# Softmax exponentials over three and two PSUM banks by turns, and VectorE's score tiles on a bank of their own

## Chip, cores, metric

One core of one Trainium2 chip. The metric is the device time in microseconds of one execution, the median of several. A run is called slow here when it is over 1.5% above the fastest of the same kernel; ratios use the other runs alone.

## The reference, cut to what matters

Two branches are mixed by a gate: a long convolution (done as a Fourier transform by matrix products) and attention with 32 query heads of size 20 over one shared key and value head. S = 2048, D = 640.

```
g = sigmoid((x * gate_w).sum(-1))
a = q * (irfft(rfft(kv) * rfft(ssm_k)) + kv * ssm_D)         # kv = shift_conv(k) * v
scores = einsum("bhqd,bkd->bhqk", q, k) * 20 ** -0.5         # 32 heads, 2048 x 2048
b = (softmax(scores) @ v).reshape(...) @ wo
out = g * a + (1 - g) * b
```

The exponentials, 32 x 2048 x 2048 of them, set the time. The convolution's matmuls are "side work", placed into TensorE's gaps. "Filler" matmuls multiply zeros and change no result; the program puts them into gaps that are left, and they are meant to keep TensorE's clock up.

## The kernel before

The program lists all operations with their dependencies; a scheduler in Python then makes a fixed order for each engine from estimated costs. TensorE executes that order strictly. Score tiles are 128 keys x 512 queries of one head, one PSUM bank each; four heads (r = 0 to 3) sit in the four row groups of 32 partitions, so four score matmuls run at once: one "burst". A PV matmul multiplies exponentials by values; PV matmuls also come in bursts, with one matmul for each head.

```python
SLACK = 0.2          # how far a side matmul may overshoot the next main burst's ready time
FILL = 0.5           # filler matmuls are placed while TensorE's busy share is below this
DVE_J = [()] * 5 + [(2, 9)] * 27     # in 27 of 32 groups, half of two key blocks' tiles go to VectorE

def busy_in(self, t, w):             # share of the last w us; `active` has one span per op
    ...                              # of cost > 0.05: a burst's last matmul, 0.25 us
# in pick_pe, when no side group fits:
    if (... self.can_fill and gap > 0.1 and self.busy_in(t, 2.4) < FILL):
        f = Op("pe", self.filler, c_mm(512), "c", "fill", 0.0)

def pairs(u):                        # ring of three pairs of banks, 0 to 5
    return (2 * u) % 3, (2 * u + 1) % 3
def QK(u, rs=(0, 1, 2, 3)): ...      # four score matmuls: one burst
def EXP(u, h):
    p, slot = pairs(u)[h], (2 * u + h) % 5          # five exp buffers
    if h == 1 and on_dve(u):
        return DEXP(u, p)                           # VectorE reads the ring's pair
    e.activation(ET[slot], ps[:, 1024 * p:1024 * p + 1024], ACT.Exp, scale=SCALE)
def PV(u): ...                       # four matmuls into bank 6, one per head
# order: EXP(u,0)  QK(u+1)  EXP(u,1)  PV(u-1)  ...      side work: bank 7
```

## Time and profile before

| | before |
|---|---|
| time, median of the 3 runs at first (range) | 930.93 us (928.56 to 932.95) |
| ScalarE busy | 97% of 928 us |
| exponentials | 970 of 128x1024 |
| score bursts | 566 (458 of four tiles, 108 of two) |
| filler matmuls during attention | 213, 67 us |
| first exponential starts, last ends | 25.5 us, 917.2 us |

The lines of the page and the chain in order of time are in the prediction and are not repeated.

### The profile page before, as it was taken

To read this page: it belongs to the slowest core of one execution; us is meant where nothing else is said; L and a number is where in the kernel's file an instruction comes from. 1 tells how busy PE (TensorE), PEld (TensorE's weight loads), DVE (VectorE), ACT (ScalarE), POOL (GpSimd) and SP (SyncE) were. 2 spreads that over 40 slices of the span, in tenths; PEclk is the share of its full clock that TensorE was granted. 3 is DMA by queue.
4 is the path that set the end of the run, shared out by engine and by line. 5 is a ranking of instruction groups with operands and counts; after the bars stand their busy time and mean duration, and the time that the engine had idled before them with its cause. 6 is when DMAs were issued, how large, how long until landed. Compare 5 with 4: busy or idle time off the path is not lost.

```text
span 928.0 us, 16257 instructions
## 1 busy us (share of the span) xinstructions
PE 804.4 (87%) x6836; PEld 333.9 (36%) x6836; DVE 615.4 (66%) x808; ACT 903.9 (97%) x994; POOL 390.3 (42%) x331
## 2 busy tenths in 40 slices
PE   6877778888998898999898899889999989888886
PEld 3222113443444333444243344333443433332222
DVE  5667884566776676776677667667657666667554
ACT  5999999999999999999999999999999999999995
POOL 2970001768724258723268325468324872000000
PEclk9999999999999999999999999999999998999898
DMA  7722542001000001000001010000000003021000
GB/s 159 256 77 85 190 130 65 13 9 40 18 19 18 13 16 33 19 19 18 18 14 30 20 53 19 18 13 9 17 19 18 13 13 95 26 69 49 20 13 28
DMA packets 40406, 41.18 MB, mean 44 GB/s; under 512 B 20147, under 2 KB 33581, under 8 KB 40333
## 3 DMA queue, kind: packets, MB, share of 16 engines
q1 hardware_dynamic: 38067, 39.56, 13.9%
q8 instruction: 53, 0.87, 0.4%
q10 hardware_dynamic: 2266, 0.59, 0.3%
q14 instruction: 20, 0.16, 0.1%
HBM read 31.76 MB, written 6.02 MB: 41 GB/s over the span
## 4 chain that ended last, share of the span: by engine, by line
ACT 93%; PE 5%; DMA 1%; SPq 1%; DVE 0%; DVEq 0%; issue 0%
ACT ET L972 93%; PE ps L956 1%; PE ps L1405 1%; PE ps L998 1%; DMA xT<-in_A_q_dram 1%; SPq L671 1%; PE ps L842 0%; PE ps L1318 0%; PE ps L898 0%; PE ps L1116 0%; PE ps L1123 0%; PE ps L1254 0%; DVE outsb L1138 0%; ACT L747 0%; PE ps L856 0%; DVEq L446 0%
## 5 line engine op out<-in xcount | busy, mean ns | idle before, releaser
L972 ACT ACTIVATE ET<-ps 128x1024 bf16<-128x1024 f32 x970 | 890.3, 1213 | 2.4 <-PE ps L956 2.0
L956 PE MATMUL ps<-qT,kT 21*128 21x512 bf16 x2048 | 224.4, 388 | 104.9 <-ACT ET L972 95.5
L1285 POOL TENSOR_TENSOR Pp<-X,K 128x512 f32<-128x512 bf16 x120 | 170.3, 1446 | 276.7 <-DVE K L1273 276.7
L998 PE MATMUL ps<-ET,vaug 128*32 128x512 bf16 x1940 | 210.0, 394 | 1.0 <-ACT ET L972 1.0
L956 PEld LDWEIGHTS ps<-qT,kT 21*128 21x128 bf16 x2048 | 56.2, 91 | 273.0 <-ACT ET L972 266.0
L986 DVE TENSOR_SCALAR dJ<-ps 128x1024 uint32<-128x1024 f32 x54 | 66.1, 1223 | 47.3 <-PE ps L956 47.2
L998 PEld LDWEIGHTS ps<-ET,vaug 128*32 128x32 bf16 x1940 | 52.3, 93 | 116.6 <-issue 112.5
L1285 POOL TENSOR_TENSOR AB<-Pp 128x256 bf16<-128x256 f32 x80 | 84.4, 1055 | 5.9
L991 DVE SCALAR_TENSOR_TENSOR dE<-dJ,dE 128x1024 f32<-128x1024 uint16 x54 | 79.4, 1471 | 0.4
L994 DVE SCALAR_TENSOR_TENSOR ETd<-dJ,dE 128x1024 bf16<-128x1024 f32 x54 | 78.1, 1446 | 0.8
L1318 PE MATMUL ps<-AB,Tcos 128*128 128x256 bf16 x320 | 76.2, 275 | 1.0 <-DVE K L1273 0.9
L993 DVE SCALAR_TENSOR_TENSOR dJ<-dJ 128x1024 f32<-128x1024 uint16 x54 | 75.1, 1391 | 0.8
L1405 PE MATMUL ps<-Tcos,zeros 128*128 128x512 bf16 x213 | 70.8, 409 | 0.0
L1318 PE MATMUL ps<-AB,Tsin 128*128 128x256 bf16 x280 | 67.3, 274 | 0.0
L1285 POOL TENSOR_TENSOR Pp<-Pp 128x512 f32<-128x512 f32 x40 | 61.3, 1532 | 3.1
L1265 DVE TENSOR_SCALAR X<-ps 128x512 bf16<-128x512 f32 x35 | 24.1, 690 | 47.1 <-PE ps L1254 46.9
L1254 PE MATMUL ps<-ssm_kT,Tsin 128*128 128x256 bf16 x320 | 49.5, 274 | 0.0
L1254 PE MATMUL ps<-kv,Tsin 128*128 128x256 bf16 x320 | 48.2, 274 | 0.0
L1254 PE MATMUL ps<-kv,Tcos 128*128 128x256 bf16 x320 | 46.7, 275 | 1.4 <-DVE kv L1181 0.5
L989 DVE TENSOR_SCALAR dE<-dJ 128x1024 uint32<-128x1024 uint32 x54 | 46.4, 860 | 1.2
L898 PE MATMUL ps<-xT,wq_pad 128*128 128x512 bf16 x160 | 44.9, 393 | 1.4 <-DVE qT L545 1.0
L1056 DVE COPY acc<-ps 128x512 f32<-128x512 f32 x31 | 21.4, 691 | 35.9 <-PE ps L998 35.4
(136 smaller groups left out, 736.5 us busy)
## 6 DMA issues: line engine op xcount, KB each, us to landing
kslab<-in_A_k_dram SPq DMA_DIRECT2D x15, 640.0 KB, 3.6
rbc<-scr_d SPq DMA_DIRECT2D x31, 256.0 KB
scr_o<-oTn SPq DMA_DIRECT2D x24, 128.0 KB
xn<-in_A_q_dram SPq DMA_DIRECT2D x4, 640.0 KB
vslab<-in_A_v_dram SPq DMA_DIRECT2D x16, 160.0 KB, 3.6
kst<-in_A_ssm_k_dram SPq DMA_DIRECT2D x5, 512.0 KB
out_dram<-outsb SPq DMA_DIRECT2D x14, 160.0 KB
oTp<-scr_o SPq DMA_DIRECT2D x12, 160.0 KB, 3.2
```

The source lines that it names most:

```text
L956: o = op("pe", lambda e, r=r, Iu=Iu, g=g, j=j, bk=banks[r]: e.matmul(self.bank(bk), T["kT4"][32 * r:32 * r + 21, 128 * j:128 * j + 128], T ...
L972: op("act", lambda e, p=p, slot=slot: e.activation(T[f"ET{slot}"][:, :], self.ps[:, 1024 * p:1024 * p + 1024], ACT.Exp, scale=SCALE), [("p ...
L986: V(lambda e, p=p: e.tensor_scalar(J[:, :], self.ps[:, 1024 * p:1024 * p + 1024], SCALE * LOG2E * 65536.0, EOFF * 65536.0, ALU.mult, ALU.add),
L989: V(lambda e: e.tensor_scalar(E[:, :], J[:, :], 7, 0x7F800000, ALU.logical_shift_left, ALU.bitwise_and), [kJ], ["dE"], c_fast(1024), **k)
L991: V(lambda e: e.scalar_tensor_tensor(Ef, lo, ED, Ef, ALU.add, ALU.mult), [kJ, "dE"], ["dE"], c_ps(1024), **k)
L993: V(lambda e: e.scalar_tensor_tensor(Jf, lo, EP, lo, ALU.add, ALU.mult), [kJ], [kJ], c_ps(1024), **k)
L994: V(lambda e: e.scalar_tensor_tensor(T["ETd"][:, :], Jf, EQ, Ef, ALU.add, ALU.mult), [kJ, "dE"], ["ETd"], c_ps(1024), **k)
L998: return op("pe", lambda e, r=r, j=j, src=src: e.matmul(self.bank(6)[32 * r:32 * r + 32, :], T["vaug"][:, j, :], src[:, 512 * (r % 2):512 ...
L1254: o = self.mm(gr, lambda e, bk, lhs=lhs, rhs=rhs, comp=comp, n=n: e.matmul(self.bank(bk, 256, 256 * comp), lhs, rhs, start=(n == 0), stop= ...
L1285: f = lambda e: e.tensor_tensor(out, a, b, alu)
L1318: self.mm(gr, lambda e, bk, lhs=lhs, fc=fc, comp=comp, h=h: e.matmul(self.bank(bk, 256, 256 * h), lhs, AB[:, fc, :, comp, :], start=(fc == ...
L1405: sch.filler = lambda e: e.matmul(self.bank(6), self.T["zeros"][:, :], self.T["Tcos"][:, 0, 0:512], start=False, stop=False)
```

## The change

The intent: each exponential instruction has a fixed cost, so fewer, wider ones save time. Six ring banks for three pairs become five, read as 3 and 2 by turns. VectorE's tiles leave the ring; their matmuls "ride" along with a score burst in a row group that is free, into bank 5 or 7, which side work shares. The five exp buffers of 1024 become two of 1536 and two of 1024, in the same memory. The two or three tiles of one exponential are called a unit.

```diff
+PATIENCE = 3.0
+SIDE = (7, 5)
-def group(self, name, prio, banks=(7,)):
+def group(self, name, prio, banks=SIDE):
-        for i in range(5):
-            sb(f"ET{i}", [128, 1024], BF16)
+        for i in range(2):
+            sb(f"ETA{i}", [128, 1536], BF16)
+            sb(f"ETB{i}", [128, 1024], BF16)
+        # stream(): all tiles in order of group G, key block j, head r, less VectorE's
+        while i < len(tiles):
+            n = 2 if len(self.units) % 2 else 3
+            self.units.append(tiles[i:i + n])
+        base = (0, 3)
+        def EXP(n):
+            lo, w = 512 * base[n % 2], 512 * len(units[n])
+            ... e.activation(et(n)[:, 0:w], self.ps[:, lo:lo + w], ACT.Exp, scale=SCALE),
+               ... [("ET", n % 4)], c_exp(w) ...
+        # DEXP: two matmuls of one tile, banks (5, 7), gr.rides = True; two VectorE reads of 512
+        # pick_pe: after a score burst, a riding group whose row is free goes first
+        for n in range(len(units)):
+            EXP(n)
+            if n + 1 < len(units):
+                QK(n + 1)
+            PVs(n - 1)        # PV groups of four tiles whose last unit is <= n - 1
```

(cut to its core)

More of the change, by code (lines that the diff above doesn't have):

```diff
@@ L24 @@
                  "cont", "nun", "succ", "ready", "start", "end", "placed", "sig", "value", "lane", "known", "seq",
-                 "banks", "last", "floating", "tail", "attached", "lat", "iss")
+                 "banks", "last", "floating", "tail", "attached", "lat", "iss", "row", "soft")
     def __init__(self, eng, fn, cost, kind, name, prio):
@@ L58, in __init__ @@
         self.iss = 0.35
+        self.row = None
+        self.soft = ()
 class Group:
     def __init__(self, banks, prio, name):
+        self.rides = False
         self.banks = banks
@@ L156, in __init__ @@
         self.active = []
+        self.rows = set()
     def busy_in(self, t, w):
@@ L191, in run @@
             op = self.pick(e, self.t[e])
-            if op is None:
+            if self.t[e] > 2000.0:
+                guard = 100001
+            if op is None or guard > 100000:
                 self.t[e] += 0.04
                 guard += 1
-                if guard > 400000:
+                if guard > 100000:
                     missing = [(o.name, o.eng) for o in g.all if not o.placed][:20]
@@ L248, in pick_pe @@
             return f
+        if self.rows and not (m is not None and m.cont):
+            best = None
+            for gr in self.gcand:
+                if gr.rides and gr.ready <= t and gr.mms[0].row not in self.rows:
+                    b = next((x for x in gr.banks if not self.bank_claimed[x] and not self.bank_busy[x]
+                              and self.bank_ready[x] <= t), None)
+                    if b is not None and (best is None or gr.prio < best[0].prio):
+                        best = gr, b
+            if best is not None:
+                gr, b = best
+                self.gcand.discard(gr)
+                gr.bank = b
+                self.bank_busy[b] = True
+                gr.mms[0].deps.update(self.bank_last[b])
+                return gr.mms[0]
         if not (m is not None and m.cont):
@@ L280, in pick_pe @@
         best = None
+        held = any(gr.rides and gr.ready <= t for gr in self.gcand)
         for gr in self.gcand:
+            if gr.rides and t - gr.ready < PATIENCE:
+                continue
             if gr.ready <= t and gr.mms[0].cost <= gap + SLACK:
@@ L284, in pick_pe @@
                 for x in gr.banks:
+                    if held and x == 5 and not gr.rides:
+                        continue
                     if not self.bank_claimed[x] and not self.bank_busy[x] and self.bank_ready[x] <= t:
@@ L305, in pick_pe @@
         _, gr, b = best
+        if gr.rides:
+            gr.mms[0].cost = 0.3
         self.gcand.discard(gr)
@@ L351, in place @@
             self.active.append((op.end - op.cost * 0.92, op.end))
+        if e == "pe":
+            if op.name != "qk":
+                self.rows = set()
+            elif op.cont:
+                self.rows.add(op.row)
+            else:
+                self.rows = {op.row}
         if op.name == "pv":
@@ L359, in place @@
                 gr.pos += 1
-                if gr.pos == len(gr.mms):
+                if gr.pos == len(gr.mms) and self.open is gr:
                     self.open = None
@@ L385, in emit @@
         for op in self.linear:
+            op.deps.difference_update(op.soft)
             drop = [d for d in op.deps if op.eng == "pe" and d.eng == "pe" and d.kind == "c"]
@@ L475, in c_fast, with c_exp @@
     return 0.16 + 0.52e-3 * n
+def c_exp(n):
+    return 0.0633 + 0.8333e-3 * n
 def c_act(n):
@@ L499, in __init__ @@
         self.crow0 = None
+        self.dqk = None
     def op(self, *a, **k):
@@ L939, in gate_fin, with stream @@
                  ["omgf"], 0.2, prio=40)
-    def attention(self, I):
+    def stream(self):
+        tiles, self.on_dve, self.pv_order = [], {}, []
+        order = (0, 1, 2, 3)
+        for G in range(8 * NB):
+            for j in range(NSC):
+                mine = order
+                if j in DVE_J[G]:
+                    mine, rest = order[:2], order[2:]
+                    self.on_dve[G, j] = tuple(sorted(rest))
+                    order = rest + mine
+                self.pv_order.append((G, j, mine))
+                tiles += [(G, j, r) for r in mine]
+        self.units, i = [], 0
+        while i < len(tiles):
+            n = 2 if len(self.units) % 2 else 3
+            self.units.append(tiles[i:i + n])
+            i += n
+        self.place_of = {t: (n, k) for n, un in enumerate(self.units) for k, t in enumerate(un)}
@@ L943, in attention, with score, et, QK @@
+    def attention(self):
         T = self.T
         op = self.op
-        N = NB * 8 * NSC
-        def pairs(u):
-            return (2 * u) % 3, (2 * u + 1) % 3
-        def QK(u, rs=(0, 1, 2, 3)):
-            Iu, g, j = u // 128, (u // 16) % 8, u % 16
-            pa, pb = pairs(u)
-            banks = (2 * pa, 2 * pa + 1, 2 * pb, 2 * pb + 1)
-            first = None
-            for r in rs:
-                o = op("pe", lambda e, r=r, Iu=Iu, g=g, j=j, bk=banks[r]: e.matmul(
-                    self.bank(bk), T["kT4"][32 * r:32 * r + 21, 128 * j:128 * j + 128],
-                    T[f"qT{Iu % 2}"][32 * r:32 * r + 21, g, :], start=True, stop=True, tile_position=(32 * r, 0)),
-                    [("kT4", j // 4), ("qT", Iu % 2, g)], [("ps", banks[r])], 0.03 if r < rs[-1] else 0.27, name="qk",
-                    main=True, cont=(r > rs[0]), banks=(banks[r],))
-                if r == rs[0]:
+        self.stream()
+        units = self.units
+        base = (0, 3)
+        started = {0}
+        def score(e, bk, G, j, r):
+            return e.matmul(self.bank(bk), T["kT4"][32 * r:32 * r + 21, 128 * j:128 * j + 128],
+                            T[f"qT{G // 8 % 2}"][32 * r:32 * r + 21, G % 8, :], start=True, stop=True,
+                            tile_position=(32 * r, 0))
+        def et(n):
+            return T["ET%s%d" % ("AB"[n % 2], n // 2 % 2)]
+        def QK(n):
+            un = units[n]
+            I = un[-1][0] // 8
+            if I not in started:
+                started.add(I)
+                self.qproj_next(I)
+                if I == NB - 1:
+                    self.g.fence(["oT3", "part"], ["xT"])
+                    self.g.fence(["wog"], ["wq_pad"])
+                    self.load_wog()
+            first = None
+            for k, (G, j, r) in enumerate(un):
+                bk = base[n % 2] + k
+                o = op("pe", lambda e, bk=bk, G=G, j=j, r=r: score(e, bk, G, j, r),
+                       [("kT4", j // 4), ("qT", G // 8 % 2, G % 8)], [("ps", bk)], 0.03 if k < len(un) - 1 else 0.27,
+                       name="qk", main=True, cont=(k > 0), banks=(bk,))
+                o.row = r
+                if k == 0:
@@ L964, in QK, with DEXP @@
                     first.deps.update(d for d in o.deps if d.eng != "pe")
-                    first.banks = tuple(banks[x] for x in rs)
-        def EXP(u, h):
-            p = pairs(u)[h]
-            slot = (2 * u + h) % 5
-            if h == 1 and on_dve(u):
-                return DEXP(u, p)
-            op("act", lambda e, p=p, slot=slot: e.activation(
-                T[f"ET{slot}"][:, :], self.ps[:, 1024 * p:1024 * p + 1024], ACT.Exp, scale=SCALE),
-                [("ps", 2 * p), ("ps", 2 * p + 1)], [("ET", slot)], 0.904, name="exp", main=True,
-                after=self.sins if u == 0 else ())
-        def DEXP(u, p):
+            first.banks = tuple(base[n % 2] + k for k in range(len(un)))
+        def EXP(n):
+            lo, w = 512 * base[n % 2], 512 * len(units[n])
+            op("act", lambda e: e.activation(et(n)[:, 0:w], self.ps[:, lo:lo + w], ACT.Exp, scale=SCALE),
+               [("ps", base[n % 2] + k) for k in range(len(units[n]))], [("ET", n % 4)], c_exp(w), name="exp", main=True,
+               after=self.sins if n == 0 else ())
+        def DEXP(G, j):
             par = self.ndexp % 2
             self.ndexp += 1
+            pr = -600.0 + 0.1 * G + 0.001 * j
             J, E, kJ = T[f"dJ{par}"], T["dE"], ("dJ", par)
@@ L983, in DEXP @@
             Ef, Jf = E[:, :].bitcast(F32), J[:, :].bitcast(F32)
-            k = dict(port=True, name="dexp", prio=-600.0 + 0.01 * u)
+            k = dict(port=True, name="dexp", prio=pr)
             V = self.dve
-            V(lambda e, p=p: e.tensor_scalar(J[:, :], self.ps[:, 1024 * p:1024 * p + 1024], SCALE * LOG2E * 65536.0,
-                                             EOFF * 65536.0, ALU.mult, ALU.add),
-              [("ps", 2 * p), ("ps", 2 * p + 1)], [kJ], c_ps(1024), prio=-8000.0, name="dexp0")
+            rs = self.on_dve[G, j]
+            for h, r in enumerate(rs):
+                gr = self.group("dqk", pr, banks=(5, 7))
+                gr.rides = True
+                w = self.g.writer.get(kJ)
+                soft = set() if h else set(self.g.readers.get(kJ, ())) | ({w} if w is not None else set())
+                self.mm(gr, lambda e, bk, r=r: score(e, bk, G, j, r), [("kT4", j // 4), ("qT", G // 8 % 2, G % 8)],
+                        0.04)
+                o = gr.mms[0]
+                o.row = r
+                if self.dqk is not None:
+                    o.deps.add(self.dqk)
+                self.dqk = o
+                o.soft = soft - o.deps
+                o.deps |= o.soft
+                self.evac(gr, "dve", lambda e, bk, h=h: e.tensor_scalar(
+                    J[:, 512 * h:512 * h + 512], self.bank(bk), SCALE * LOG2E * 65536.0, EOFF * 65536.0, ALU.mult,
+                    ALU.add), (), [kJ], c_ps(512))
             V(lambda e: e.tensor_scalar(E[:, :], J[:, :], 7, 0x7F800000, ALU.logical_shift_left, ALU.bitwise_and),
@@ L997, in PVmm @@
         def PVmm(r, j, src, key, late=False, **k):
-            return op("pe", lambda e, r=r, j=j, src=src: e.matmul(
-                self.bank(6)[32 * r:32 * r + 32, :], T["vaug"][:, j, :], src[:, 512 * (r % 2):512 * (r % 2) + 512],
+            return op("pe", lambda e: e.matmul(
+                self.bank(6)[32 * r:32 * r + 32, :], T["vaug"][:, j, :], src,
                 start=(j == 0), stop=(j == NSC - 1), tile_position=(0, 32 * r)),
                 [key, "vaug", ("vaugb", j // 4)], [] if late else [("ps", 6)], name="pv", **k)
-        def PV(u):
-            j = u % 16
-            rs = (0, 1) if on_dve(u) else (0, 1, 2, 3)
-            for r in rs:
-                slot = (2 * u + r // 2) % 5
-                o = PVmm(r, j, T[f"ET{slot}"], ("ET", slot), cost=0.03 if r < rs[-1] else 0.27, main=True,
-                         cont=(r > 0), banks=(6,))
-                o.last = j == NSC - 1
-                if j == 0:
-                    self.pv0 = o
-                if o.last and r == 0:
-                    o.deps.update(self.late_pv)
-                    self.late_pv = []
-            if on_dve(u):
-                a = PVmm(2, j, T["ETd"], "ETd", late=True, cost=0.03, after=[self.pv0])
-                b = PVmm(3, j, T["ETd"], "ETd", late=True, cost=0.27)
-                a.floating = True
-                a.tail = (b,)
-                b.deps.add(a)
-                b.attached = True
-                self.late_pv += [a, b]
@@ L1025, in on_dve @@
-        def on_dve(u):
-            return u % 16 in DVE_J[u // 16]
-        lo, hi = I * 128, I * 128 + 128
-        if I == 0:
-            QK(0)
-        for u in range(lo, hi):
-            if u + 1 < N:
-                if (u + 1) % 128 == 0:
-                    self.qproj_next(I + 1)
-            EXP(u, 0)
-            split = on_dve(u)
-            if u + 1 < N:
-                QK(u + 1, (0, 1) if split else (0, 1, 2, 3))
-            EXP(u, 1)
-            if I == 0 and u == 40:
-                self.gate_fin()
-            if u > 0:
-                PV(u - 1)
-                if u % 16 == 0:
-                    self.norm((u - 1) // 128, ((u - 1) // 16) % 8)
-            if split and u + 1 < N:
-                QK(u + 1, (2, 3))
@@ L1049, in attention, with PV @@
-        if hi == N:
-            PV(N - 1)
+        def PV(G, j, rs):
+            pv0 = None
+            for k, r in enumerate(rs):
+                n, q = self.place_of[G, j, r]
+                o = PVmm(r, j, et(n)[:, 512 * q:512 * q + 512], ("ET", n % 4), cost=0.03 if k < len(rs) - 1 else 0.27,
+                         main=True, cont=(k > 0), banks=(6,))
+                o.last = j == NSC - 1
+                if k == 0:
+                    first = o
+                    if o.last:
+                        o.deps.update(self.late_pv)
+                        self.late_pv = []
+                else:
+                    first.deps.update(d for d in o.deps if d.eng != "pe")
+            if j == 0:
+                for jd in DVE_J[G]:
+                    DEXP(G, jd)
+                    ra, rb = self.on_dve[G, jd]
+                    a = PVmm(ra, jd, T["ETd"][:, 0:512], "ETd", late=True, cost=0.03, after=[o])
+                    b = PVmm(rb, jd, T["ETd"][:, 512:1024], "ETd", late=True, cost=0.27)
+                    a.floating = True
+                    a.tail = (b,)
+                    b.deps.add(a)
+                    b.attached = True
+                    self.late_pv += [a, b]
@@ new lines, in attention, with PVs @@
+        todo = list(self.pv_order)
+        def PVs(n):
+            while todo and max(self.place_of[todo[0][0], todo[0][1], r][0] for r in todo[0][2]) <= n:
+                G, j, rs = todo.pop(0)
+                PV(G, j, rs)
+                if j == NSC - 1 and G < 8 * NB - 1:
+                    self.norm(G // 8, G % 8)
+        QK(0)
+        for n in range(len(units)):
+            EXP(n)
+            if n + 1 < len(units):
+                QK(n + 1)
+            if n == 64:
+                self.gate_fin()
+            PVs(n - 1)
@@ L1052, in norm @@
+        PVs(len(units))
     def norm(self, I, g):
@@ L1389, in build @@
         self.kshift()
-        for I in range(NB):
-            if I == NB - 1:
-                self.g.fence(["oT3", "part"], ["xT"])
-                self.g.fence(["wog"], ["wq_pad"])
-                self.load_wog()
-            self.attention(I)
+        self.attention()
         self.g.fence(self.late_fams, self.early_fams)
```

## The prediction

> **What bounds the kernel now.** I read the busy shares first, then the waits by engine, then the chain in order of time.
>
> ```profile
> PE 804.4 (87%) x6836; PEld 333.9 (36%) x6836; DVE 615.4 (66%) x808; ACT 903.9 (97%) x994; POOL 390.3 (42%) x331
> ...
> PEclk9999999999999999999999999999999998999898
> ...
> L972 ACT ACTIVATE ET<-ps 128x1024 bf16<-128x1024 f32 x970 | 890.3, 1213 | 2.4 <-PE ps L956 2.0
> L956 PE MATMUL ps<-qT,kT 21*128 21x512 bf16 x2048 | 224.4, 388 | 104.9 <-ACT ET L972 95.5
> ...
> L986 DVE TENSOR_SCALAR dJ<-ps 128x1024 uint32<-128x1024 f32 x54 | 66.1, 1223 | 47.3 <-PE ps L956 47.2
> ...
> L1405 PE MATMUL ps<-Tcos,zeros 128*128 128x512 bf16 x213 | 70.8, 409 | 0.0
> ```
>
> ScalarE is busy 97% of 928 us, and 970 exponentials make up 890 of it. It idles 2.4 us before them, while the score matmuls (L956) idle 105 us waiting for them. TensorE's 87% is not tightness: 71 us of it is filler (L1405) that only keeps its clock up.
>
> The chain in order of time gives the pace, the one number that matters:
>
> ```profile
> 25.48 75.26 ACT ET L972 x82
> 100.83 17.43 ACT ET L972 x19
> ...
> 122.86 414.44 ACT ET L972 x452
> ...
> 548.40 218.32 ACT ET L972 x238
> ...
> 768.02 0.62 PE ps L956 x4
> 768.64 1.02 ACT ET L972
> ```
>
> 414.44/452 = 0.917 us and 218.32/238 = 0.917 us per exponential over hundreds in a row. The few breaks (near 119, 540, 768, 869, 908) add up to little: from the first end (26.5) to the last (917.2) are 890.7 us for 969 steps; 969 x 0.9167 = 888.3. So 2.4 us are lost in all, most of it where matmuls run at half clock (0.62 us instead of 0.39).
>
> The records of one exponential are longer than the pace:
>
> ```profile
> L972 ACT ACTIVATE ET<-ps x970: 1017/1222/1332, 25.5 to 916.1; 128x1024 bf16<-128x1024 f32 x194
> ```
>
> Minimum 1.017 us, median 1.222, maximum 1.332 against a pace of 0.917: records overlap, and a start may come up to 0.3 us late before the end moves. In the start times I see starts 0.98 or 1.08 us apart while the ends stay 0.917 apart (945 of 969 end steps are 915 to 919 ns). A stall must exceed that elasticity to cost anything, so I count in ends.
>
> **What the Trainium skill says.** "ScalarE: Activation LUTs", What ACT_TABLE_LOAD costs: an activation with immediate scale and bias takes 186 ns + 0.833 ns per element, and neighbours overlap by about 93, so a fixed 93 ns per instruction. "Perfetto Trace Analysis", Optimizing Scalar/DVE Operations: the fixed part is about 51 ns where ScalarE reads PSUM. The trace: 917 - 1024 x 0.833 = 64 ns, between the two. No view of before has another width on PSUM, so whether 64 ns is all fixed isn't shown. "TensorE: Matmul & The Clock Gate", Why this matters for your kernels: matmuls of K=32 in different row groups run concurrently, starts 4 ns or less apart. The trace agrees: four score matmuls of 512 columns have 0.39 us of busy time together, their starts 3 to 4 ns apart. So a burst of 3 or 2 costs TensorE about as much as one of 4. The same page, Part 1: the clock halves when activity is low; the trace has such dips (the 8s above).
>
> **The change, part by part.**
>
> 1. *Fewer exponentials.* Attention has 4 x 8 x 16 x 4 = 2048 score tiles of 128x512; VectorE takes 54 x 2 = 108, as before. ScalarE keeps 1940: before 970 instructions of 2, after 388 of 3 and 388 of 2, so 776. Elements are the same; 194 fixed parts go. If all 64 ns are fixed: 194 x 64 = 12.4 us. If 51 are and the rest goes with the elements: 9.9. I take 11.8. Everything here is on the path. Expected pace: 1536 x 0.833 + 64 = 1.344 us and 0.917, by turns, 2.26 for five tiles.
>
> 2. *Ring of five banks, only double buffered.* Score burst n+1 waits for exponential n-1. From the trace: a burst starts 0.055 us after the end it waits for; an exponential that waits just for it starts 0.455 after the burst starts; its shortest record is 1.017, for three banks 1.017 + 0.427 = 1.444. So end to end over two exponentials at least 0.055 + 0.455 + 1.444 = 1.95 us against 2.26: slack 0.31. Before: 1.53 against 1.83, slack also 0.31. Same tightness, 388 such places (before 485): no loss.
>
> 3. *Four exp buffers instead of five.* Exponential n overwrites the buffer of n-4. Five tiles are two units, and a PV group of four consecutive tiles spans three units where it begins on a unit's third tile (position 2 modulo 5). There the group reads n-4 to n-2, and it stands in TensorE's order behind score burst n. With 60 tiles per group G, starts at 22 and 52 fit, 2 x 27; the first five G (64 tiles, 16 places in 320) give 16: 70 in all. Chain there: 0.055 + score burst 0.32 (start of burst to start of PV in the timeline, 400.02 to 400.34) + 0.455 + 1.444 = 2.27 against 2.26: zero slack. Each costs 0.01 plus whatever holds the burst up. A quarter of the bursts of before start 0.1 to 0.3 us late (side matmuls, late PV pairs); mean some 0.04. So 70 x 0.05 = 3.5 us, less where the delay falls elsewhere: 2.5 us.
>
> 4. *VectorE's tiles on a bank of their own.* 108 reads of 512 at 0.69 us (rows of that form, as the eviction acc, show 691 ns) for 54 of 1.223: 74.6 - 66.1 = +8.5 us on an engine at 66%: beside. Their matmuls ride in a free row group: almost nothing. The split bursts of before go. ScalarE's ring no longer waits for VectorE's read; at most a few tenths of a us come of that, as little is lost there.
>
> 5. *TensorE.* Score bursts 776 for 566, at about 0.3 us: +63 us. Per five tiles: 2 x 0.3 + 1.25 x 0.33 = 1.0 of 2.26 us. That comes out of filler (71 us) and idle time (13% of 928 = 124 us). Side work gets a second bank, so I expect no delay; GpSimd, which ends the convolution, is done some 150 us before the end in the slices. Beside the path.
>
> Sum: 930.9 - 11.8 + 2.5 = 921.6. Start (25.5 us) and tail (928.0 - 917.2 = 10.8 us) are the same instructions. I take 921 us.
>
> **Rivals.**
>
> A. *The buffer wait takes the place of the overhead.* If the elasticity of 0.3 us is not there for three-bank instructions, or the PV waits stack up (a late PV pair in front adds 0.22 us), each of the 70 costs 0.2 to 0.25 us: 14 to 18 us, and the time is 931 to 936. For it: the static order was made with a TensorE to ScalarE latency of 0.12 us, and the trace shows more. Against it: ends kept pace in before through 0.06 to 0.15 us of late starts.
>
> B. *TensorE cold.* Less filler and bursts on 2 or 3 row groups instead of 4 could let the clock halve more often. With 0.62 us matmuls the normal loop still fits (2.17 of 2.26), but the 70 tight places then lose 0.45 each and filler in front of a burst more. In the quiet last 150 us that is 3 to 8 us: 924 to 930; if it spreads over the whole kernel, 950. For it: all large losses of before are such dips. Against: bursts come every 1.13 us instead of 1.83, and filler is still placed below half activity.
>
> C. *Side order worse.* TensorE executes in order, so a side matmul that waits for VectorE in one of the shared banks blocks score bursts. Before has about 5 us of such waits, none reaching ScalarE. A bad order costs 5 us or more: 925 to 945. Two side banks speak against it.
>
> D. *All goes well:* 12.4 off, the 2.4 lost before saved as well: 916. More isn't there: 2% faster would be 912.3.
>
> **Range and chances.** Steps 1 and 3 give 917 to 925; A, B and C pull upwards only. I give D and near it a quarter, the middle half, and A to C together a quarter, most of that still within 2% (below 949.5). Range 916 to 931. Faster by over 2% would need more than step 1 can give: 0.02. Slower by over 2% only through B or C spreading: 0.05.
>
> **What would show it.** Right: 776 exponentials; the chain's long stretches with 2.26 us per pair of instructions (1.13 per instruction); two forms with shortest records near 1.44 and 1.02 us; ScalarE busy near 878 us in L972's successor and idle before it below 4 us; first exponential still near 25.5. Step 3 wrong: pieces of the chain through PV matmuls every 16 us or so, or waits of ScalarE for PV. B: PEclk digits of 8 and below in more slices. C: ScalarE waiting over 1 us at a time behind TensorE waits for VectorE. The prediction is wrong if the pace per pair is over 2.27 (a cost per bank or per element in the 64 ns), or if long waits of ScalarE sum to over 8 us.

## More of the kernel before

One more view is needed later, the busy time of each engine in two stretches. Columns: stretch, its length, busy time and count of each engine, clock granted to TensorE, DMA share, GB/s.

```profile
120.00:180.00 60.00, 49.55 (x431) 19.82 (x430) 33.16 (x58) 59.98 (x67) 18.69 (x18) 0.98 0.23 63
230.00:290.00 60.00, 54.92 (x492) 25.23 (x489) 43.03 (x49) 60.00 (x67) 29.63 (x21) 1.00 0.05 15
```

In both, ScalarE runs 67 instructions in 60 us and is never idle.

## The result

998.54 us median (986.69 to 1001.72, 4 runs), against 929.74 of the kernel before: ratio 1.0694, 95% interval 1.0592 to 1.0796. A ratio is the mean time of one kernel's fast runs over that of the other's of the same rounds, so not quite the ratio of the medians. The profiled run (1001.72 us) is called slow by the 1.5% rule, but two of the fast runs, 997.16 and 999.93, are within half a per cent of it, with granted clocks of 0.893 and 0.884 against its 0.886; it stands for the rest.

The page of the kernel after, the lines that answer to those of before:

```profile
PE 931.3 (93%) x6734; PEld 346.0 (35%) x6780; DVE 605.7 (61%) x862; ACT 909.8 (91%) x800; POOL 385.4 (39%) x331
...
PEclk9969855899999999999979999887999689995776
...
L1048 ACT ACTIVATE ETA<-ps 128x1536 bf16<-128x1536 f32 x388 | 567.9, 1464 | 64.8 <-PE ps L1016 38.6
L1048 ACT ACTIVATE ETB<-ps 128x1024 bf16<-128x1024 f32 x388 | 402.8, 1038 | 4.2 <-PE ps L1016 2.8
L1016 PE MATMUL ps<-qT,kT 21*128 21x512 bf16 x2048 | 335.8, 422 | 47.1 <-ACT ETA L1048 29.8
```

ScalarE's records shrank to their shortest form: a mean of 1464 and 1038 ns, close to the shortest of 1451 and 1016. No queue stands in front of it any more; it waits. Its clock line has runs of 5 to 8 where before had a few 8s near the end. The waits of ScalarE, longest first (total us, times, longest):

```profile
ACT ETA L1048 <- PE ps L1016: 38.6, 51, 1.8
ACT ETA L1048 <- PE ps L1090: 22.2, 39, 2.3
```

L1016 is the score matmul, L1090 the PV matmul. Both waits stand before the three-bank exponential. The same two stretches as before:

```profile
120.00:180.00 60.00, 57.56 (x260) 13.52 (x261) 34.80 (x58) 47.61 (x40) 0.89 (x1) 0.50 0.29 94
230.00:290.00 60.00, 55.58 (x461) 23.16 (x460) 42.42 (x52) 58.84 (x53) 52.60 (x39) 1.00 0.09 28
```

At full clock (230 to 290), 53 exponentials in 60 us are 1.13 us each, the pace that was predicted. From 120 to 180 the clock is 0.50 throughout, TensorE is busy 57.56 of 60 us with only 260 matmuls, and ScalarE gets 40 exponentials done.

**Where the time went.** I took the end of each exponential in the trace and summed how much each step exceeds its undisturbed value (1.343 us for three banks, 0.917 for two; the medians are 1.344 and 0.916). A step counts as cold where over 30% of it lies in a stretch that the clock record gives as half speed.

| | before | after |
|---|---|---|
| undisturbed sum | 889 us | 877 us |
| cold time during attention | 24 us | 222 us |
| loss in cold steps | 1.3 us | 61.1 us |
| loss in steps at full clock | 0.9 us | 26.2 us |

So the fewer exponentials did save 12 us, and 87 us were lost in front of them. 61 of these lie where TensorE ran at half clock, 26 at full clock. The 70 places where a PV group spans three units can be counted off from the program: 53 of them, at full clock, lost 13.7 us, 0.258 each, and the 257 other three-bank exponentials at full clock lost 12.9, or 0.050 each. In the cold the 16 places lost 14.7 us, 61 other three-bank exponentials 40.0 (0.66 each), the two-bank ones 6.3. In the cold the score burst takes 0.53 us to the next matmul in place of 0.32, a side matmul of 256 columns 0.213 in place of 0.109.

Before the change the filler rule placed 213 filler matmuls; now it places 157. The trace of the kernel after has records of only 128 of these, and the expectation of e1 below was written with that number. Each filler has a weight load of its own; no weight load is missing in any trace here, as a count of the built programs shows. So fillers are counted by weight loads from here on (first the kernel before, then the one after):

```profile
L1405 PEld LDWEIGHTS ps<-Tcos,zeros 128*128 128x128 bf16 x213 | 15.2, 99 | 33.6 <-issue 30.9
...
L1488 PEld LDWEIGHTS ps<-Tcos,zeros 128*128 128x128 bf16 x157 | 12.7, 103 | 36.6 <-issue 35.6
```

### The profile page after: what moved, and what is told of

Same layout as the page of the kernel before. It is cut to its first block, busy times and chain, and to the rows that moved or that the text cites. A ratio compares the mean times of both kernels' runs of the same rounds, so it can differ in the third digit from the quotient of the medians.

```text
span 999.9 us, 15908 instructions
## 1 busy us (share of the span) xinstructions
PE 931.3 (93%) x6734; PEld 346.0 (35%) x6780; DVE 605.7 (61%) x862; ACT 909.8 (91%) x800; POOL 385.4 (39%) x331
## 4 chain that ended last, share of the span: by engine, by line
PE 63%; ACT 33%; DVE 1%; issue 1%; DMA 1%; SPq 1%; DVEq 0%
ACT ETA L1048 21%; PE ps L1016 19%; PE ps L1090 13%; PE ps L1342 13%; ACT ETB L1048 12%; PE ps L1406 8%; PE ps L1488 4%; PE ps L942 3%; PE ps L1180 1%; PE ps L1440 1%; DMA xT<-in_A_q_dram 1%; PE ps L958 1%; SPq L715 0%; PE ps L886 0%; PE ps L1288 0%
## 5 line engine op out<-in xcount | busy, mean ns | idle before, releaser
L1048 ACT ACTIVATE ETA<-ps 128x1536 bf16<-128x1536 f32 x388 | 567.9, 1464 | 64.8 <-PE ps L1016 38.6
L1048 ACT ACTIVATE ETB<-ps 128x1024 bf16<-128x1024 f32 x388 | 402.8, 1038 | 4.2 <-PE ps L1016 2.8
L1016 PE MATMUL ps<-qT,kT 21*128 21x512 bf16 x2048 | 335.8, 422 | 47.1 <-ACT ETA L1048 29.8
L1090 PE MATMUL ps<-ETB,vaug 128*32 128x512 bf16 x776 | 220.1, 429 | 0.1
L1090 PE MATMUL ps<-ETA,vaug 128*32 128x512 bf16 x1164 | 211.3, 429 | 0.3 <-DVE acc L1144 0.3
L1016 PEld LDWEIGHTS ps<-qT,kT 21*128 21x128 bf16 x2048 | 76.6, 92 | 276.3 <-ACT ETA L1048 104.6
L1078 DVE TENSOR_SCALAR dJ<-ps 128x512 uint32<-128x512 f32 x108 | 74.4, 689 | 49.2 <-PE ps L1016 48.5
L1090 PEld LDWEIGHTS ps<-ETA,vaug 128*32 128x32 bf16 x1164 | 48.4, 94 | 78.5 <-issue 75.0
L1090 PEld LDWEIGHTS ps<-ETB,vaug 128*32 128x32 bf16 x776 | 49.1, 94 | 54.7 <-issue 54.3
L1342 PE MATMUL ps<-ssm_kT,Tcos 128*128 128x256 bf16 x320 | 52.8, 278 | 0.7 <-DVE dJ L1078 0.4
```

What stands on the lines that cost most here:

```text
L1016: return e.matmul(self.bank(bk), T["kT4"][32 * r:32 * r + 21, 128 * j:128 * j + 128], T[f"qT{G // 8 % 2}"][32 * r:32 * r + 21, G % 8, :], ...
L1048: op("act", lambda e: e.activation(et(n)[:, 0:w], self.ps[:, lo:lo + w], ACT.Exp, scale=SCALE), [("ps", base[n % 2] + k) for k in range(le ...
L1078: self.evac(gr, "dve", lambda e, bk, h=h: e.tensor_scalar(J[:, 512 * h:512 * h + 512], self.bank(bk), SCALE * LOG2E * 65536.0, EOFF * 6553 ...
L1090: return op("pe", lambda e: e.matmul(self.bank(6)[32 * r:32 * r + 32, :], T["vaug"][:, j, :], src, start=(j == 0), stop=(j == NSC - 1), ti ...
L1342: o = self.mm(gr, lambda e, bk, lhs=lhs, rhs=rhs, comp=comp, n=n: e.matmul(self.bank(bk, 256, 256 * comp), lhs, rhs, start=(n == 0), stop= ...
```

## Experiments

Sixteen kernels ran. First the theories:

- **Clock.** Filler fell, because the rule counts a burst of two or three tiles like one of four, and there are more bursts. TensorE falls to half clock, is then too slow for the loop, and stays there.
- **Buffer wait.** The PV group over three units, with four buffers, and the stall before the exponential that needs its buffer.
- **TensorE full.** More bursts, each with a change between tiled and full matmuls around it, leave no room for the side work that shares TensorE.

All are correct but e10 and e15. "Cold" and "loss" are computed as above, from the profiled run, slow for e1, e2, e4, e5 and e14. The medians are over all runs, the ratios over the fast ones. The kernel before has 213 fillers.

| | kernel | fillers | median us | ratio to before | cold us | loss cold / full clock |
|---|---|---|---|---|---|---|
| | after | 157 | 998.5 | 1.069 | 222 | 61.1 / 26.2 |
| e1 | after, filler limit 0.7 | 368 | 954.9 | 1.025 | 75 | 25.5 / 28.7 |
| e2 | after, filler by tiles | 247 | 970.4 | 1.036 | 107 | 32.3 / 27.6 |
| e3 | after, PV group split | 120 | 968.9 | 1.045 | 138 | 32.5 / 21.2 |
| e4 | e2 + e3 | 220 | 945.1 | 1.014 | 65 | 20.6 / 19.9 |
| e5 | e4, overshoot 0.1 us | 220 | 936.0 | 0.999 | 65 | 18.9 / 17.5 |
| e6 | e4, limit 0.6 | 334 | 936.4 | 1.008 | 10 | 3.7 / 21.1 |
| e7 | after, all units of two | 90 | 1519.0 | 1.632 | 1472 | 593 / 0 |
| e8 | before, filler limit 0.3 | 63 | 951.1 | 1.024 | 132 | 16.3 / 4.9 |
| e9 | e6, overshoot 0.1 us | 318 | 935.7 | 1.006 | 10 | 3.1 / 18.6 |
| e10 | e6, less side work (wrong) | 433 | 943.4 | 1.015 | 27 | 13.3 / 14.0 |
| e11 | e6, least gap 0.3 us | 230 | 936.4 | 1.004 | 41 | 13.8 / 11.0 |
| e12 | e5, limit 0.55 | 266 | 946.2 | none | 0 | 0 / 17.8 |
| e13 | e11, limit 0.7 | 280 | 928.7 | 0.999 | 41 | 14.5 / 12.0 |
| e14 | e11, limit 1.0 | 300 | 927.8 | 0.997 | 44 | 14.4 / 13.8 |
| e15 | e13, less side work (wrong) | 360 | 930.7 | 1.000 | 48 | 16.3 / 5.0 |
| e16 | e13, rule looks back 1.2 us | 286 | 937.4 | 1.008 | 0 | 0 / 15.1 |

### e1, e2: more filler

```diff
e1: -FILL = 0.5
    +FILL = 0.7
e2:      if e == "pe" and op.cost > 0.05: self.active.append((op.end - op.cost * 0.92, op.end))
    now, for score and PV bursts:
    +    self.tiles = self.tiles + 1 if op.cont or op.attached else 1
    +    self.active.append((op.end - 0.2475 * self.tiles / 4, op.end))
```

> The changed kernel with only the filler limit raised from 0.5 to 0.7, so the static order puts more filler matmuls into TensorE's gaps. Clock theory (61 of the 87 us lost before exponentials fall in stretches at half clock, because filler fell from 213 to 128): cold time falls from 222 us to under 40 us, and the time from 998 to about 940 to 955 us. Buffer-wait theory (the 70 places with four exp buffers and the double-buffered ring cost the time, and the cold clock is a result of the stalls): time stays above 980 us. In-the-way theory (TensorE is full at 93 percent): more filler makes it slower, over 1005 us.

> The changed kernel, the filler rule alone altered: a burst of score or PV matmuls counts as busy in proportion to its number of 32-row or 32-column tiles (a quarter each of a full matmul's time), not as a full matmul whatever its size. Clock theory: some 40 to 90 more fillers, most cold stretches gone (under 60 us of the 222), time 935 to 960 us. If only the buffer waits matter: within 1 percent of 998.

e1: 954.9 us, as the clock theory said (940 to 955), though with 75 us cold rather than under 40. More filler on a TensorE that is 93% busy made the kernel 44 us faster, so filler is not "in the way" there, and a time above 980 didn't come. Loss at full clock stays as it was (28.7). The four runs of e1 go with the clock: 948.07 us at 0.986, 953.13 at 0.979, 956.71 at 0.975, 966.88 at 0.961. e2: 970.4, above its range of 935 to 960; 107 us cold. Counting by tiles is a step in the right direction and not enough. Its order has 247 fillers, more than the 213 of the kernel before, and still 107 us were cold: the number of fillers alone does not say how long TensorE is cold. That the miscounted bursts are why filler fell follows from the rule in the code; that the clock governor itself measures something like filled area is not shown.

### e3, e4: the PV group over three units split

```diff
-                PV(G, j, rs)
+                PV(G, j, rs[1:] if (G, j) in early else rs)
+            if todo:
+                G, j, rs = todo[0]
+                at = [self.place_of[G, j, r][0] for r in rs]
+                if at[0] <= n and max(at) - at[0] == 2 and j > 0 and (G, j) not in early:
+                    early.add((G, j))
+                    PV(G, j, rs[:1])
```

> The changed kernel with the PV group that spans three exponential units split: its first tile, from the buffer that is needed next, goes out with the group before. Buffers, filler rule and exponentials are the same. Buffer-wait theory: waits of ETA exponentials for PV (22 us) go to below 4 us and the time falls by 15 to 30 us. Clock theory: the fall is 5 to 15 us, as cold stretches stay at 150 to 250 us.

> Filler rule by tile count and split PV group together. If the two causes are separate and together the whole: both gone, about 920 to 930 us, at or below the kernel before. If a third cause (side order, shared banks) is at work: above 940.

e3: 968.9, 30 us less, the upper end of what the buffer-wait theory allowed. Waits of exponentials for PV fall from 22.2 us to 0.3; what is left for ETA is nearly all the score matmul:

```profile
ACT ETA L1048 <- PE ps L1016: 31.6, 52, 1.8
```

At full clock the places where a group spanned three units lose 0.030 us each in place of 0.258, 1.8 us in all; the other three-bank exponentials lose more, 0.071 each in place of 0.050, so that the sum at full clock fell by 5 us only. The larger part of the 30 came with the cold time, 222 to 138 us, though the order has fewer fillers than without the split (120 for 157). So the two causes are coupled: fewer stalls, and less cold time with less filler. e4 puts both together: 945.1, not the 920 to 930 of "two causes and no third". Over 940 was the mark for a third cause.

### e7, e8: the clock by itself

```diff
e7: -            n = 2 if len(self.units) % 2 else 3
    +            n = 2
    -        base = (0, 3)
    +        base = (0, 2)
e8 (on the kernel before): -FILL = 0.5
                           +FILL = 0.3
```

> The changed kernel with all units of two tiles (ring of 2 x 2 banks, 970 exponentials of 1024 again, 970 score bursts), everything else of the change kept: VectorE's tiles on their own bank, side work on two banks, four buffers. If the three-bank exponentials are at fault, this is near 930. If the many small score bursts are (TensorE time, and filler counted wrongly for them), it is as slow as the changed kernel or slower, 990 to 1050, with more cold time than 222 us.

> The kernel before with the filler limit lowered from 0.5 to 0.3, nothing else. Clock theory: it too falls into cold stretches of tens of us, in total 100 us or more, and gets slower, by 10 to 40 us (940 to 970); the loss is smaller than in the changed kernel as it has one score burst per 1.83 us. Rival (cold clock is harmless without the smaller ring): cold, but within 5 us of 930.

e7 keeps the change's own bank, side banks and double-buffered ring, but goes back to exponentials of 1024. It has 970 bursts of two tiles, and 90 fillers. The clock line of its page:

```profile
PEclk9555555555555555555555555555555555555555
```

From 34 us on, for 1475 us, TensorE ran at half clock, 98% busy, and the kernel took 1519 us, far beyond what I expected (990 to 1050). The harm does not need three-bank exponentials. Nor did TensorE get warm here by being busy all the time, as the profile counts busy time: 60 us from 230 on hold 59.94 us of it at clock 0.50:

```profile
230.00:290.00 60.00, 59.94 (x275) 18.42 (x274) 22.98 (x33) 36.91 (x38) 32.28 (x29) 0.50 0.03 8
```

e8 changes one number in the kernel before. Fillers fell from 213 to 63 (the line below has the 40 that the trace recorded), the cold time rose from 24 to 132 us, and it lost 22 us (951.1), in the middle of the 940 to 970 expected:

```profile
PEclk8989758999999998999999999999999998998586
...
L1405 PE MATMUL ps<-Tcos,zeros 128*128 128x512 bf16 x40 | 18.9, 518 | 2.3 <-issue 2.3
```

That shows the clock as a cause in the kernel before; in the kernel after, e1 showed it, where the filler limit alone was changed and the loss in cold steps fell from 61.1 to 25.5 us.

### e5, e6, e9, e12: what is left at full clock

```diff
e5, e9, e12: -SLACK = 0.2        e6, e9: -FILL = 0.5        e12: -FILL = 0.5
             +SLACK = 0.1                +FILL = 0.6             +FILL = 0.55
(all on top of e4)
```

> As the filler-by-tiles and split kernel (945 us), with the overshoot that the static order allows side matmuls before a score burst cut from 0.2 to 0.1 us. Theory of the full TensorE (what is left of warm loss, 20 us, is side matmuls that hold the three-tile score burst 0.44 us after the end it waits for, over the slack of 0.31): warm loss falls to 5 to 12 us and the time to 930 to 938 us. Rival (bank or VectorE waits in the in-order queue): no change, 945 within 5.

> As the filler-by-tiles and split kernel, with the filler limit at 0.6. Clock theory: the last cold stretch (65 us from 115 on) is gone or under 15 us, and with it about 15 to 20 us: 925 to 932 us. If filler is by now in the way: warm loss grows above 30 us and the time stays at 945 or more.

> Filler by tiles with limit 0.6, split group and overshoot 0.1 us together. Cold time below 15 us as with the 0.6 alone; warm loss 15 to 18 us as with the 0.1 alone. Time 926 to 933 us, so equal to the kernel before within 1 percent. A cold stretch of 50 us in some runs (theory: the smaller overshoot leaves gaps) would show as runs over 940.

> As filler by tiles, split group and overshoot 0.1, with filler limit 0.55 between the 0.5 that left a 58 us cold stretch in half of the runs and the 0.6 that has none. Time 924 to 932 us; if filler and side matmuls now compete for the same gaps, it is within 3 us of the 0.6 kernel.

e6 took the cold time to 10 us and still took 936.4, over its 925 to 932: 21 us are lost at full clock. The same stretch that was cold is now at full speed, and TensorE is busy 57 of 60 us:

```profile
120.00:180.00 60.00, 57.14 (x429) 20.95 (x429) 38.30 (x62) 59.94 (x53) 8.58 (x7) 1.00 0.31 97
```

The overshoot (e5, e9) matters little: 17.5 and 18.6 us, where 5 to 12 and 15 to 18 were expected. e5 took 936.0 as expected (930 to 938), e9 935.7 (926 to 933 expected). A piece of e4's timeline shows one late burst (start, length, engine):

```profile
438.17 1.45 ACT L1053 ACTIVATE ETA<-ps 128x1536 bf16<-128x1536 f32 x1
...
438.66 0.39 PE L1021 MATMUL ps<-qT,kT 21*128 21x512 bf16 x2
438.98 0.94 PE L1354 MATMUL ps<-ssm_kT,Tcos 128*128 128x256 bf16 x7
439.52 1.02 ACT L1053 ACTIVATE ETB<-ps 128x1024 bf16<-128x1024 f32 x1
439.75 0.38 PE L1354 MATMUL ps<-ssm_kT,Tsin 128*128 128x256 bf16 x2
440.07 0.39 PE L1021 MATMUL ps<-qT,kT 21*128 21x512 bf16 x3
...
440.56 1.45 ACT L1053 ACTIVATE ETA<-ps 128x1536 bf16<-128x1536 f32 x1
```

The exponential ETA of 438.17 ends at 439.62; the burst of three that waits for it starts at 440.07, 0.45 us later, because nine side matmuls stand before it; the next ETA starts 2.39 us after the last instead of 2.26. TensorE never pauses. From start to start, a side matmul of 256 columns takes 0.109 us, but 0.205 where a score burst follows: the change from full to tiled matmuls costs 0.096 us that the static order doesn't know. How TensorE's time during attention is used, each matmul counted until the next one starts (53 of e6's 334 fillers have no record, so its filler is somewhat more and another row less):

| | before | e6 |
|---|---|---|
| score bursts | 186 us | 258 us |
| PV bursts | 191 us | 200 us |
| side matmuls | 337 us | 335 us |
| filler | 67 us | 80 us |
| idle | 111 us | 29 us |

e12 (924 to 932 expected) came out at 929.83 at a clock of 0.999 and 944 to 950 at 0.967 to 0.978; with a single fast run it has no ratio.

### e10, e11, e13, e14, e15, e16: room on TensorE

```diff
e11: +MINGAP = 0.3
     +        if gap < MINGAP: return None        # no side matmul or filler in short gaps
e10, e15 (wrong result): -            for fc in range(NF):     # inverse transform, NF = 8
                         +            for fc in range(4):
e13: FILL = 0.7   e14: FILL = 1.0   e16: busy_in(t, 1.2) in place of 2.4   (on top of e11)
```

> Wrong result on purpose: filler by tiles with limit 0.6 and split group, and the inverse transform adds up 4 of its 8 frequency blocks, so 320 of the 640 matmuls of 256 columns there (some 35 us of TensorE) are gone; all else is the same. Theory of the full TensorE: with that room the warm loss falls from 21 us to 10 to 14 us, and the time to 922 to 929 us, though filler takes part of the room. Rival (each loss is a wait on VectorE or on banks): 936 within 3.

> Filler by tiles with limit 0.6 and split group; besides, no side matmul and no filler is placed where the gap before the next main burst is under 0.3 us in the static order, so fewer changes between bursts and full matmuls, each of which takes about 0.1 us more. Full TensorE theory: side matmuls in the same number with fewer changes, warm loss 8 to 14 us; but the filler falls to about that of the kernel with limit 0.5, so 20 to 60 us cold: 925 to 945 us.

> Filler by tiles, split group and the least gap of 0.3 us, filler limit raised to 0.7 (in the kernel with 0.6 a 41 us cold stretch stayed and cost 14 us, warm loss was 11). If warm loss came down there through fewer changes between bursts and full matmuls: warm loss stays 9 to 14 us, cold time falls below 10 us, time 918 to 925 us, faster than the kernel before by about 1 percent. If it came down only because there was less filler: warm loss is back at 17 to 21 us, time 928 to 935.

> The same with filler limit 1.0, so filler wherever a gap of 0.3 us is. Cold time zero. If filler in long gaps is harmless: as with 0.7 within 4 us. If filler itself delays bursts: warm loss over 15 us, 926 to 934.

> Wrong result on purpose: the kernel with least gap and limit 0.7, with half of the inverse transform's matmuls left out. Full TensorE theory: with 35 us less side work and few changes the warm loss falls to 4 to 9 us, and where the clock holds the time comes to 913 to 920 us, near ScalarE's floor. Rival (the warm loss is inherent to the double-buffered ring, whatever TensorE has to do): warm loss as in the kernel with full side work, within 2 us.

> As the kernel with filler by tiles, split group, least gap and limit 0.7, with the filler rule looking back 1.2 us instead of 2.4. In the traces the cold stretch from 115 us on begins in a lull right after five dense projection matmuls: the rule that looks back 2.4 us still counts them and places no filler for two bursts. If that is how the stretch begins, the short window puts filler there, the cold stretch is gone in all runs (clock 0.99 and up) and the time is 923 to 928 us with no run over 932, a little below the kernel before. Otherwise some runs show clocks of 0.98 and 936 to 942 us as before.

The loss at full clock follows the room on TensorE. From 21.1 (e6) it falls to 14.0 (10 to 14 expected) with half of the inverse's matmuls gone (e10), and to 12.0 with fewer changes between side work and bursts, though there are still 280 fillers (e13; in 447 places a side matmul runs right up to a score burst, e6 had 496); with both it is 5.0 (e15; 4 to 9 expected). Less filler alone does not explain it: e4 has 220 and loses 19.9, e11 has 230 and loses 11.0. Whether it is the fewer changes that help is not shown, as they fell by a tenth only. If the double-buffered ring itself were at fault, e15 would have stayed where e13 is. The times don't follow as cleanly: e10 took 943 (922 to 929 expected), e13 928.7 (918 to 925 expected) and e15 930.7 (913 to 920 expected), since a cold stretch, mostly one of 27 to 48 us, came in the profiled run of each. Where the clock held, e13 took 925.94 (0.999), e14 925.58 (1.000) and e15 923.07 (0.989). e11, at 936.4 us with 41 us cold, came as expected (925 to 945, 20 to 60), and e14 was within 4 us of e13, as expected if filler in long gaps is harmless.

e16 tested how that stretch begins. It missed: half of its six runs had clocks of 0.971 to 0.979 and took 940 to 948 us. The short look back put no filler into the lull that I had in mind, so how the stretch begins stays untested.

No version is clearly better than the kernel before: e14, the best, has a ratio of 0.9972 (0.994 to 1.0003).

## Why the prediction was wrong, by its own steps

1. **Fewer exponentials: right.** 388 of 1.343 us and 388 of 0.917. Fixed 64 ns for both widths, so 12.4 us saved, the upper of the two values I weighed.
2. **Double-buffered ring, slack 0.31: the figure right, its use wrong.** The shortest three-bank record is 1451 ns (1.444 predicted). But the slack is there for a burst that starts 0.055 us after the end it waits for; with TensorE full it started 0.45 us after it in the place shown from e4.
3. **Four buffers, 70 tight places: mechanism right, size too small.** The count of 70 was right. I allowed 0.05 us each, 2.5 in all; at full clock each lost 0.258 (13.7 in all), and the split brought that to 0.030. With a chain of zero slack all lateness counts in full, and I had taken the lateness (0.04 us mean) from a kernel with more room on TensorE. (The trace has some 15% of the bursts over 0.1 us late, not a quarter; the mean is right.)
4. **VectorE's tiles: right as far as seen.** 108 reads of 689 ns, 74.4 us (74.6 predicted); no waits of ScalarE for VectorE appear.
5. **TensorE: this is the step that failed.** The burden was sized well: +63 us predicted for the score bursts, +72 measured in e6. "That comes out of filler (71 us) and idle time ... Beside the path" is what was wrong. The work was not beside the path: of the 87 us lost in front of exponentials, 61.1 lie at half clock, and at full clock 12.9 at three-bank exponentials where no buffer was tight. Filler is not free room: with 63 fillers in place of 213, the kernel before was cold for 132 us and took 951 (e8). And idle time was not free either: in e6, with 10 us cold, it is 29 us for 111 before, and 21.1 us were lost at full clock; with half of the inverse's matmuls gone and a least gap, 5.0 (e15).

**Rival B** (cold TensorE) was the outcome: I had written "if it spreads over the whole kernel, 950", and gave slower by over 2% a chance of 0.05. Against it I had said that "filler is still placed below half activity". That trusted the rule's count, in which a burst of two tiles is as busy as one of four: filler fell from 213 to 157. The size was off because I let only the 70 tight places and filler in front of bursts lose at half clock ("the normal loop still fits"). The tight places lost 0.92 each there (0.45 predicted). In the cold stretches 40.0 of the 61 us were lost by three-bank exponentials elsewhere: 40 instructions in the 60 us from 120 on are 3.0 us a pair, against 2.26. Bursts take 1.7 times and side matmuls twice as long there, and TensorE as a whole, busy for 57.56 of these 60 us, no longer fits. **Rival A** (buffer wait, "0.2 to 0.25 us" each) came as well, with 0.258 (by the prediction's own sums 919.1 us and 14 to 17.5 make 933 to 937, not 931 to 936). **Rival C** (side order) does not show: TensorE's waits for VectorE, but for one of 3 us at the start, are 6.5 us in all in the kernel after and 5.0 in the kernel before.

**Still open:** what exactly the clock governor measures, why a stretch begins in one execution and not in the next of the same kernel, and how the loss of 61 us would divide between stalls that start a cold stretch and the cold that prolongs them. The runs show only that fewer stalls went with less cold time (e3), and that the stalls are longer in the cold (0.92 us for 0.258 at a tight place). More filler does not always help either: e2 with 247 was cold for 107 us, e12 with 266 in one of four runs not at all.

## What to carry to other kernels

Before counting an engine's idle time or filler as room, ask what the filler is for and how the rule that places it counts; recount it for the new shape of work. A half-clock stretch can last although TensorE is busy (65 us in the kernel after, 1475 in e7), so the margin has to hold at the worst moment, not on average. Splitting the same matmul work into more, smaller tiled bursts cost TensorE in full per burst, not per tile: 0.33 us each for 566 bursts (before) and for 776 (e6), the change between full and tiled matmuls included.

## What the Trainium skill lacked or had wrong

- "TensorE: Matmul & The Clock Gate", Part 1, ties the half clock to an idle window of some 3.4 us and the full clock to a busy one. Here it stayed at 0.50 for 1475 us with TensorE 98% busy by the profile (e7), and for 65 us in the kernel after. The steps in the clock record, but for those that the trace cuts, are multiples of 3.41 us and only full and half occur, as the page says.
- "Perfetto Trace Analysis", Optimizing Scalar/DVE Operations, gives about 51 ns of fixed cost for ScalarE on PSUM. The sustained pace here has 64 ns, at 1024 and at 1536 columns alike; the shortest start-to-start step, 904 ns, is 51 above 1024 x 0.833.
- No page has the elasticity of a saturated ScalarE: a start up to 0.3 us late left the ends 917 ns apart (record 1.017 us when it waits, up to 1.332 when it doesn't).
- "TensorEngine Tiling (Array Packing)", Key Properties, says that a change of tiling mode drains TensorE, but no page has a time for it: 0.096 us here from full to row-tiled (0.205 from start to start against 0.109).
